# A delta-rule attention with a low-rank mixer on one core: fronts by token tile, other transfer times in the order model, and a new order

## The chip, the cores and the metric

The kernel runs on one core of a Trainium2 chip. A core has five engines that each work through their own queue of instructions in order: TensorE (PE, matrix multiply; PEld is its weight load), VectorE (DVE), ScalarE (ACT), GpSimd (POOL) and SyncE (SP). They wait for one another by semaphores. Transfers between the chip's memory (HBM) and the on-chip memory (SBUF) are issued by SP, ACT and POOL and carried by 16 DMA engines. Results of matmuls land in PSUM. The metric is the device time of one execution in microseconds.

## The reference

Four batches, eight heads, 768 positions, 48 numbers per head. The delta rule gives `x`, a mixer with a rank-32 token mix and a two-layer channel mix gives the output. Everything is float32; `U`, `V`, `w_ch1`, `w_ch2` come as float64 and are read by the kernel as pairs of 32-bit words.

```python
for t in range(S):
    kt, vt, bt = (k_n[:, :, t], v[:, :, t], beta[:, :, t, None])
    y[:, :, t] = np.einsum('bhd,bhde->bhe', q[:, :, t], state)
    v_old = np.einsum('bhde,bhd->bhe', state, kt)
    state = state + bt[:, :, :, None] * np.einsum('bhd,bhe->bhde', kt, vt - v_old)
...
h = xt @ U @ V                       # x: (4, 768, 384), heads side by side
u = x + h.transpose(0, 2, 1)
ch = np.maximum(u @ w_ch1, 0.0) @ w_ch2   # 384 -> 1536 -> 384
return (u + ch).astype(np.float32)
```

## The kernel before

**Delta rule.** The work is cut into eight units `n`: unit `2b` is the first half (384 positions) of batch `b`, unit `2b+1` the second, each of six chunks of 64 positions. A unit is loaded by `load` (L361 to L391, its issues at L379: k, q, v and a second copy z of some keys, in pieces of 72 KB; for units 2 to 7 half of the pieces go through POOL's queue). `grams` turns keys and queries with TensorE transposes (L475), copies them (L490) and multiplies them (L502); `blocks` solves small triangular systems on VectorE (L584, then pairs of L593 and L599, then L606 and L615) and joins the blocks with small matmuls (L649, L663, L689, L692, L707, L710), with a correction on VectorE (L667). `norms` scales by the key norms and by v (L458). Two units share each of two places in SBUF (`slot0`, `slot1`), so unit n+2 can be loaded only when unit n is done.

**Recursion.** `recur(b)` runs the twelve chunks of a batch one after the other: `prepare` (L808, L819), then for every chunk pb (L857), z (L870, VectorE), the state's increment (L885) and the state s (L895, VectorE), and beside this the outputs (L772, L786), which ScalarE puts into `X` (L756).

**Mixer.** For each batch the 768 positions go in three channel groups `i` of 256 positions, two token tiles `c` of 128 each. `front(b, i)` makes `u`: once per batch T (L1180, with a copy `tt`, L1186), then H (L1198), an addition on VectorE (L1202), transposes (L1207) and a copy to `ut` (L1209). `wide(b, i)` then multiplies by w_ch1 (L1288, called W1 below; six pairs of blocks of features), applies the relu (L1231) and multiplies by w_ch2 (L1328) in seven products instead of eight, with sums on VectorE (L1251, L1258) and the results added to `X` (L1264). The last batch has its first layer done in seven products too (`quick`, L1085). `load_weights` brings in 14 slices of the weights as 64-bit words (L967) and converts each with five VectorE operations (L989 to L1017) and one of ScalarE (L974); the sums of w_ch2 (L925) follow the last two slices.

**What sets the order.** The program is written as many small parts (Python generators), each yielding the operations that it wants next. `run` keeps a model of the engines' clocks while the program is built: among the parts that can go on, it takes the one that comes soonest, and among those about equally soon the one with the smaller rank. The result is a fixed order of instructions in each engine's queue; on the chip nothing is chosen any more. Three things enter: the costs that the parts give with their operations, the landing times that `landing` works out for transfers, and the ranks, which the calls of `begin` give and the table `PLACES` overrides by name.

Of the kernel before, what the change touches and what calls it, by code (L numbers as in the profile page):

```python
# [19 lines left out]
GT = 256  # L20
# [6 lines left out]
def kernel(  # L27
# [66 lines left out]
    def dve(n):  # L94
        return (n + 151) / 960.0

    def act(n):
        return 0.16 + n / 1200.0
# [14 lines left out]
    def emitted(key, after=0.0):  # L113
        done[key] = state["now"] + after
        for i in awaited.pop(key, ()):
            missing[i].discard(key)
            if not missing[i]:
                woken.append(i)

    def landing(packets, each=0.0235):  # L120
        state["hw"] = max(state["hw"], state["now"] + 1.0) + packets * each / 16
        return state["hw"] + 0.4 - state["now"]

# [14 lines left out]
            waits[i] = s  # L138

    PLACES = """  # L140
    add_up b1 i1 45.09; blocks n3 111.0; blocks n4 92.42; blocks n6 79.19
    front b1 i2 64.0; front b2 i2 68.2; grams n1 i1 1.0; grams n3 i0 53.42
    grams n3 i1 -4.5; grams n4 i0 45.18; joins n0 h1 45.17; joins n1 h0 15.27
    joins n2 h0 -4.0; joins n2 h1 7.5; joins n5 h1 18.5; joins n6 h0 60.13
    joins n6 h1 68.5; joins n7 h1 62.0; last_sum b0 i2 80.69; load n0 nameq halves(0, 1) 75.0
    load n0 namez halves(0, 1) 3.5; load n1 namez halves(0, 1) 92.5; load n5 namek halves(0, 1) 49.53; load n5 namez halves(0, 1) 92.89
    load n6 namek halves(0, 1) 68.35; load_beta u0 51.5; load_beta u1 90.62; load_weights 88.45
    norms n1 113.0; norms n2 108.5; norms n3 19.33; norms n5 46.0
    outputs b0 c0 94.0; outputs b0 c3 15.7; outputs b0 c5 84.5; outputs b1 c6 56.12
    outputs b2 c0 87.54; outputs b2 c5 58.09; outputs b3 c0 -10.5; outputs b3 c1 51.03  # L150
    outputs b3 c4 81.5; outputs b3 c6 78.5; prepare n0 h0 99.5; prepare n0 h1 78.37
    prepare n1 h0 80.0; prepare n2 h0 -1.5; prepare n2 h1 6.5; prepare n3 h0 8.5
    prepare n5 h0 7.5; prepare n5 h1 44.42; prepare n6 h1 43.06; products n0 i0 j0 97.01
    products n0 i0 j1 82.0; products n0 i1 j1 110.0; products n1 i1 j1 53.69; products n2 i0 j1 73.87
    products n3 i0 j1 31.11; products n4 i0 j0 55.59; products n4 i0 j1 57.63; products n4 i1 j0 57.63
    products n5 i1 j1 3.5; products n6 i0 j1 100.7; products n6 i1 j0 73.37; products n6 i1 j1 47.56
    products n7 i1 j0 59.09; products n7 i1 j1 86.0; recur b0 31.68; recur b1 19.99
    recur b3 22.0; seed n6 -8.0; start i1 113.77; wide b0 i0 65.24
    wide b0 i2 73.0; wide b1 i2 115.5; wide b2 i1 76.0
    """  # L160
    PLACES = dict(x.strip().rsplit(" ", 1) for x in PLACES.replace("\n", ";").split(";") if x.strip())

# [106 lines left out]
    def pair(x):  # L269
        return P[:, BANK["pair"][x] : BANK["pair"][x] + 2]  # L270
# [90 lines left out]
    def load(n, name, halves):  # L361
        kn, _, _, _, qn, vn, _, kz = units[n]
        t, src = dict(k=(kn, k), q=(qn, q), v=(vn, v), z=(kz, k))[name]
        b, hf = divmod(n, NU)
        yield need(("rec", n - 2), *[("x", b - 1, UC * hf + c) for c in range(UC)])
        if name == "v":
            yield need(("turned", n))
        if name == "k" and n == 0:
            e = "sp" if halves == (0,) else "act"
        else:  # L370
            e = "sp"
        for g in halves:
            if n >= NU and g:
                e = "pool"
            queue = dict(sp=nc.sync, act=nc.scalar, pool=nc.gpsimd)[e]
            for s in range(1, 4, 2) if name == "z" else range(4):
                to = dict(k=s, q=s, v=s % 2 * 2 + s // 2, z=s // 2)[name]
                yield op(e, 0.65, port=False)
                queue.dma_start(  # L379
                    out=t[half(1 - g if name == "z" else g), :, to, 0:D],  # L380
                    in_=src[b, 4 * g + s, hf * UC * L : (hf + 1) * UC * L, :].rearrange(
                        "(c t) d -> t c d", t=L
                    ),
                )
                after = landing(384)
                if name == "z" or s % 2:
                    emitted((name, n, g, s // 2), after)
        if len(halves) == 1 and halves[0]:
            yield op("act", 1.6)
            nc.scalar.sqrt(warm, warm)  # L390
# [162 lines left out]
    def halves(t, split):  # L553

        size = BK // split
        flat = t.rearrange("p a b -> p (a b)")[:, 0 : split * size * (BK + (split > 1))]
        return flat.rearrange("p (u x) -> p u x", u=split)[:, :, 0 : size * BK].rearrange(
            "p u (a b) -> p u a b", b=BK
        )[:, :, :, 0:size]
# [371 lines left out]
    def load_weights():  # L931
# [14 lines left out]
        def start(i):  # L946
            _, src, kind = slices[i]
            n = size(i)
            before = max([x for x in range(i) if where[x] == where[i]], default=-1)
            yield need(("started", i - 1), ("freed", before), *[("joined", 0)] * (where[i] == 2))  # L950
            to = wides[where[i]][:, 0 : 2 * n]
            landed[i] = to.rearrange("p (n two) -> p n two", two=2)
            src = src.bitcast(I32)
            if kind == "c":
                pieces = [(to.rearrange("p (c r) -> p c r", c=NB), src.rearrange("(c p) r -> p c r", c=NB))]
            elif kind == "a":
                to = to.rearrange("p (t f x) -> p t f x", t=KT, f=2)
                pieces = [(to[:, :, f], src[:, :, f]) for f in range(2)]
            elif kind == "f":
                to = to.rearrange("p (a f d) -> p f a d", a=2, f=2)  # L960
                pieces = [(to[:, f], src[f]) for f in range(2)]
            else:
                pieces = [(to[quarter(j)], src) for j in range(128 // R)]
            e, queue = ("pool", nc.gpsimd) if i < 1 else ("sp", nc.sync)
            for to, of in pieces:
                yield op(e, 0.6, port=False)
                queue.dma_start(out=to, in_=of)  # L967
            emitted(("started", i))
            emitted(("wide", i), landing(256, 0.13) + 0.6)

        def raised(i, power):
            cost = 0.16 + size(i) * 0.001
# [197 lines left out]
    def front(b, i):  # L1170
        yield need(
            ("front", *before(b, i)), *[("wide", *before(*before(b, i)))] * (b < LAST),
            ("weights", 1), *[("x", b, c) for c in range(NC)],
        )
        x = X[:, b % 2]
        if i == 0:
            o = yield op("pe", 0.8, "T", take="pair", words=24)
            p_t = one(o)[:, 0:DM]
            for c in range(NB):
                nc.tensor.matmul(  # L1180
                    p_t[R * (c % 4) : R * (c % 4) + R], u_sb[:, c], x[:, c],
                    start=(c < 4), stop=(c + 4 >= NB),
                )
            yield op("dve", dve(384), give=[("pair", o)])
            tts[b] = mix.tile([128, DM], FP32, name="tt", bufs=1)
            nc.vector.tensor_copy(out=tts[b], in_=p_t)  # L1186
        tt = tts[b]
        cs = list(range(i * GT // 128, (i + 1) * GT // 128))
        if b < LAST:
            ut = uts[b, i] = mix.tile([128, KT, GT], FP32, name="ut")  # L1190
        else:
            ut = ut_last[:, :, GT * i : GT * i + GT]

        at = slice(cs[0], cs[-1] + 1)
        o = yield op("pe", 1.3, "F", take="pair", words=8)
        p_h = pair(o)[:, :, 0:DM]
        for m, c in enumerate(cs):
            nc.tensor.matmul(  # L1198
                p_h[:, m], v_sb[:, c * 128 : (c + 1) * 128], tt, start=True, stop=True
            )  # L1200
        yield op("dve", dve(768), give=[("pair", o)])
        nc.vector.tensor_tensor(out=x[:, at], in0=x[:, at], in1=p_h, op=ALU.add)  # L1202
        o = yield op("pe", 0.84, "F", take="pair", words=12, flow=0.64)
        p_u = pair(o)[:, :, 0:DM].rearrange("p m (t n) -> p m t n", t=KT)
        for m, c in enumerate(cs):
            for t in range(KT):
                nc.tensor.transpose(p_u[:, m, t], x[:, c, t * 128 : (t + 1) * 128], ident)  # L1207
        yield op("act", act(768), give=[("pair", o)])
        nc.scalar.copy(ut.rearrange("p t (m n) -> p m t n", m=NT), p_u)  # L1209
        emitted(("front", b, i), 0.1)  # L1210

    def reserve():
# [180 lines left out]
```

## Time and profile before

| | us |
|---|---|
| median of three runs (615.25 to 617.24) | 617.05 |
| the profiled execution | 622.36 |
| its span, first to last instruction | 620.6 |
| PE busy in the span | 584.3 (94%) |
| DVE busy | 418.3 (67%) |
| ACT busy | 235.6 (38%) |
| POOL busy | 81.5 (13%) |
| mean TensorE clock | 0.929 of full |

The profile is of one execution. Matmuls overlap in the array, so a busy PE need not be at its peak; a float32 matmul appears as two records in the trace. "Idle before" is the time an engine stood still ahead of an instruction, with what ended it. Of the time, the chain of waits gives 84% to TensorE, 7% to VectorE and 2% to transfers.

### The profile page before, as it was taken

The page shows a single profiled execution, that of the slowest core. Times are in us where ns is not written, and L with a number is a line of the kernel's source. Part 1 is how long each engine was busy: PE and PEld are TensorE (multiplying, and loading weights), DVE is VectorE, ACT ScalarE, POOL GpSimd, SP SyncE. Part 2 cuts the span into 40 slices and gives each one's busy share as a digit, 9 for nine tenths or more (in the row PEclk, how much of TensorE's full clock was granted, in tenths as well). Part 3 has the DMA queues.
Part 4 walks back from the last instruction along what each step waited for, and adds up shares of the span by engine and source line. Part 5 has one row for each costly group of instructions (what it writes and reads, how often), then busy time and mean ns, then how long its engine had stood idle before and what let it go on. Part 6 is the DMA issues. An engine that isn't in the chain of part 4 may idle for free.

```text
span 620.6 us, 23281 instructions
## 1 busy us (share of the span) xinstructions
PE 584.3 (94%) x10452; PEld 502.8 (81%) x10452; DVE 418.3 (67%) x1000; ACT 235.6 (38%) x462; POOL 81.5 (13%) x145
## 2 busy tenths in 40 slices
PE   5767968899999999999999999999999999999997
PEld 4666967689889889788988978988989878755997
DVE  6968979688988817899887359968972235132542
ACT  4735654651044174246327323353134131244000
POOL 3001006410000230151025032010010000000000
PEclk9766565799999999999999999999999999999999
DMA  6560549940000240370034043000000000000001
GB/s 125 107 160 5 170 154 201 207 107 2 27 5 3 61 65 4 69 131 4 3 74 91 3 96 57 11 29 3 3 28 2 27 2 2 25 2 0 6 36 36
DMA packets 72293, 33.26 MB, mean 54 GB/s; under 512 B 59649, under 2 KB 70657, under 8 KB 72193
## 3 DMA queue, kind: packets, MB, share of 16 engines
q1 hardware_dynamic: 66400, 24.98, 18.1%
q0 software_dynamic: 4192, 6.49, 4.9%
q8 instruction: 82, 1.34, 0.9%
q10 hardware_dynamic: 1600, 0.30, 0.3%
q14 instruction: 19, 0.15, 0.1%
HBM read 27.03 MB, written 4.72 MB: 51 GB/s over the span
## 4 chain that ended last, share of the span: by engine, by line
PE 84%; DVE 7%; issue 3%; ACT 2%; DMA 2%; SPq 2%; DVEq 0%; ACTq 0%
PE P L1328 27%; PE P L1288 23%; PE P L1085 7%; PE P L502 4%; PE P L475 3%; PE P L1198 3%; PE P L857 3%; DMA slot<-in_k_dram 2%; PE P L808 2%; PE P L819 2%; PE P L885 2%; PE P L772 2%; SPq L379 2%; PE P L1207 1%; PE P L786 1%
## 5 line engine op out<-in xcount | busy, mean ns | idle before, releaser
L1288 PE MATMUL P<-ut,w_sb 128*128 128x256 f32 x648 | 153.8, 386 | 0.0
L1288 PEld LDWEIGHTS P<-ut,w_sb 128*128 128x128 f32 x648 | 119.6, 191 | 19.0 <-issue 1.9
L1328 PE MATMUL P<-w_sb,hs 128*128 128x192 f32 x540 | 95.1, 330 | 0.0
L1328 PEld LDWEIGHTS P<-w_sb,hs 128*128 128x128 f32 x540 | 87.3, 190 | 1.6
L599 DVE TENSOR_TENSOR xt<-xt,prod 128x112 f32<-128x112 f32 (+21 forms) x200 | 64.5, 323 | 6.9
L1264 DVE TENSOR_TENSOR X<-X,P 128x192 f32<-128x192 f32 x84 | 29.6, 352 | 58.4 <-PE P L1328 57.3
L756 ACT COPY X<-P 64x192 f32<-64x192 f32 x96 | 30.1, 314 | 101.9 <-PE P L786 99.7
L593 DVE TENSOR_TENSOR prod<-gs,xt 128x112 f32<-128x112 f32 (+21 forms) x200 | 63.9, 320 | 4.5
L1231 ACT ACTIVATE hs<-P 128x512 f32<-128x512 f32 x54 | 32.2, 597 | 82.0 <-PE P L1288 78.6
L1328 PE MATMUL P<-w_sb,S 128*128 128x192 f32 x288 | 50.2, 329 | 0.0
L1328 PEld LDWEIGHTS P<-w_sb,S 128*128 128x128 f32 x288 | 46.7, 190 | 0.5
L475 PE MATMUL P<-ident,slot 128*128 128x128 f32 x192 | 31.5, 314 | 11.2 <-DMA slot<-in_k_dram 7.4
L870 DVE TENSOR_TENSOR z<-slot,P 128x192 f32<-128x192 f32 x44 | 15.5, 353 | 35.2 <-PE P L857 32.2
L728 ACT COPY slot<-zz 32x384 f32<-32x384 f32 x64 | 32.5, 509 | 14.9 <-DVE X L1264 8.6
L475 PEld LDWEIGHTS P<-ident,slot 128*128 128x128 f32 x192 | 25.9, 162 | 14.6 <-issue 8.1
L502 PEld LDWEIGHTS P<-slot 48*64 48x64 f32 x1536 | 28.8, 151 | 6.9 <-ACT slot L490 3.2
L502 PE MATMUL P<-slot 48*64 48x64 f32 x1536 | 32.4, 238 | 1.7 <-ACT slot L490 1.4
L1085 PE MATMUL P<-slot,w_sb 128*128 128x384 f32 x96 | 33.3, 486 | 0.0
L379 POOL DMA_DIRECT2D slot<-in_k_dram x36 | 23.6, 669 | 66.8 <-PE P L885 66.0
L1328 PE MATMUL P<-w_sb,slot 128*128 128x192 f32 x180 | 30.1, 326 | 0.0
L1328 PEld LDWEIGHTS P<-w_sb,slot 128*128 128x128 f32 x180 | 29.4, 190 | 0.5
L490 ACT COPY slot<-P 128x768 f32<-128x768 f32 x30 | 23.5, 801 | 16.5 <-PE P L475 14.4
(143 smaller groups left out, 888.1 us busy)
## 6 DMA issues: line engine op xcount, KB each, us to landing
out_dram<-X SPq DMA_DIRECT2D x22, 192.0 KB, 1.8
slot<-in_k_dram SPq DMA_DIRECT2D x56, 72.0 KB, 3.8
X<-in_moe_w_ch_dram SPq DMA_DIRECT2D x10, 384.0 KB, 5.1
wide<-in_moe_w_ch_dram SPq DMA_DIRECT2D x10, 384.0 KB, 5.3
slot<-in_q_dram SPq DMA_DIRECT2D x40, 72.0 KB, 3.7
slot<-in_v_dram SPq DMA_DIRECT2D x40, 72.0 KB, 3.2
slot<-in_k_dram POOLq DMA_DIRECT2D x36, 72.0 KB, 4.5
slot<-in_q_dram POOLq DMA_DIRECT2D x24, 72.0 KB, 5.2
```

Source lines behind the costliest of these rows:

```text
L379: queue.dma_start(out=t[half(1 - g if name == "z" else g), :, to, 0:D], in_=src[b, 4 * g + s, hf * UC * L : (hf + 1) * UC * L, :].rearrang ...
L475: nc.tensor.transpose(p_t[:, c // 3, c % 3], t[:, c, 2 * j : 2 * j + 2].rearrange("p s d -> p (s d)"), ident,)
L502: nc.tensor.matmul(p_g[half(g ^ (par * i)), par, c], kq[rows, c, j, 0, half(g)], kq[rows, c, j, i, half(g)], start=True, stop=True,)
L593: nc.vector.tensor_tensor(out=prod, in0=gb[:, :, j : j + 1, j + 1 :].to_broadcast([128, split, m, w]), in1=xb[:, :, 0:m, j : j + 1].to_bro ...
L599: nc.vector.tensor_tensor(out=xb[:, :, 0:m, j + 1 :], in0=xb[:, :, 0:m, j + 1 :], in1=prod, op=ALU.subtract,)
L728: nc.scalar.copy(pg[quarter(i), :, at, :, a : a + BK], cut(zc, h)[quarter(i)].rearrange("p r (c j) t -> p r c j t", j=2),)
L756: nc.scalar.copy(x[half(c % 2), c // 2, 4 * D * g : 4 * D * (g + 1)].rearrange("p (j r d) -> p r j d", r=2, d=D), states(p_y)[half(g)],)
L1085: nc.tensor.matmul(to, w, t, start=start, stop=stop, skip_group_check=True)
L1231: nc.scalar.activation(hs[:, fs[0] : fs[1] + 1 : fs[1] - fs[0]], p_f, ACTF.Relu)
L1264: nc.vector.tensor_tensor(out=to, in0=to, in1=p, op=ALU.add)
L1288: nc.tensor.matmul(p_f[:, fs.index(f)], w1_sb[:, y, 256 * t + 128 * fs.index(f) :][:, 0:128], ut[:, t], start=(t == 0), stop=(t == KT - 1),)
L1328: nc.tensor.matmul(p_o, a[:, f], w2_sb[:, w, f], start=(first and f == 0), stop=(f == HF - 1), skip_group_check=True,)
```

## The change

Three edits. First, `front` handles each token tile by itself: one H matmul, one addition of 384 columns, three transposes and one copy of 384 columns, each tile in a PSUM bank of its own, as two parts that the order model may place apart (before: both tiles in one go, with one addition and one copy of 768). Second, the model gets other times of transfers: 0.0215 in place of 0.0235 us per packet of a load of q, k or v, 0.45 or 0.15 us added by queue; and for the weights 0.095 per packet and piece in place of 0.13 per slice. Third, the whole table of ranks is another one.

```diff
-    def landing(packets, each=0.0235):
+    def landing(packets, each=0.0215):
         state["hw"] = max(state["hw"], state["now"] + 1.0) + packets * each / 16
...
-                after = landing(384)
+                after = landing(384) + (0.45 if e == "pool" else 0.15)
...
                 queue.dma_start(out=to, in_=of)
+                after = landing(256, 0.095)
             emitted(("started", i))
-            emitted(("wide", i), landing(256, 0.13) + 0.6)
+            emitted(("wide", i), after + 0.2)
...
-        at = slice(cs[0], cs[-1] + 1)
-        o = yield op("pe", 1.3, "F", take="pair", words=8)
-        p_h = pair(o)[:, :, 0:DM]
-        for m, c in enumerate(cs):
+        def block(c):
+            o = yield op("pe", 0.65, "F", take="pair", words=4)
+            p_h = one(o)[:, 0:DM]
             nc.tensor.matmul(
-                p_h[:, m], v_sb[:, c * 128 : (c + 1) * 128], tt, start=True, stop=True
+                p_h, v_sb[:, c * 128 : (c + 1) * 128], tt, start=True, stop=True
             )
-        yield op("dve", dve(768), give=[("pair", o)])
-        nc.vector.tensor_tensor(out=x[:, at], in0=x[:, at], in1=p_h, op=ALU.add)
-        o = yield op("pe", 0.84, "F", take="pair", words=12, flow=0.64)
-        p_u = pair(o)[:, :, 0:DM].rearrange("p m (t n) -> p m t n", t=KT)
-        for m, c in enumerate(cs):
+            yield op("dve", dve(384), give=[("pair", o)])
+            nc.vector.tensor_tensor(out=x[:, c], in0=x[:, c], in1=p_h, op=ALU.add)
+            o = yield op("pe", 0.56, "F", take="pair", words=6, flow=0.32)
+            p_u = one(o)[:, 0:DM].rearrange("p (t n) -> p t n", t=KT)
             for t in range(KT):
-                nc.tensor.transpose(p_u[:, m, t], x[:, c, t * 128 : (t + 1) * 128], ident)
-        yield op("act", act(768), give=[("pair", o)])
-        nc.scalar.copy(ut.rearrange("p t (m n) -> p m t n", m=NT), p_u)
+                nc.tensor.transpose(p_u[:, t], x[:, c, t * 128 : (t + 1) * 128], ident)
+            at = c * 128 - i * GT
+            yield op("act", act(384), give=[("pair", o)])
+            nc.scalar.copy(ut[:, :, at : at + 128], p_u)
+            emitted(("ut", b, c))
+
+        for c in cs:
+            begin(block(c), 2)
+        yield need(*[("ut", b, c) for c in cs])
         emitted(("front", b, i), 0.1)
...
     PLACES = """
-    add_up b1 i1 45.09; blocks n3 111.0; blocks n4 92.42; blocks n6 79.19
-    front b1 i2 64.0; front b2 i2 68.2; grams n1 i1 1.0; grams n3 i0 53.42
...
+    add_up b1 i0 84.69; block b0 i0 c0 76.5; block b0 i0 c1 76.5; block b0 i2 c4 76.5
+    block b0 i2 c5 76.5; block b1 i2 c4 75.8; block b2 i1 c2 29.12; block b2 i2 c4 75.5
...
     """
```

In the built programs all five queues change their order. SP's first transfers are k and z of unit 0, q 0, k 1, two pieces of q 1, v 0, the rest of q 1, z 1, v 1 (before: k and z 0, k 1, q 1, q 0, one piece of z 1, v 1 and v 0). On TensorE, the first W1 matmuls stand ahead of the turnings of unit 3 (before: behind part of them), and the blocks of unit 2 start after 18 W1 matmuls (before: after the first group's 36 and its second layer). On VectorE, eleven of the 14 weight slices and all but one operation of a twelfth are converted ahead of the last z of batch 0 (before: ten), and the blocks of unit 2 come ahead of the last two slices (before: behind them).

More of the change, by code (lines that the diff above doesn't have):

```diff
@@ L140 @@
     PLACES = """
-    add_up b1 i1 45.09; blocks n3 111.0; blocks n4 92.42; blocks n6 79.19
-    front b1 i2 64.0; front b2 i2 68.2; grams n1 i1 1.0; grams n3 i0 53.42
[L143 to L158, printed above, removed]
@@ L159 @@
-    wide b0 i2 73.0; wide b1 i2 115.5; wide b2 i1 76.0
+    add_up b1 i0 84.69; block b0 i0 c0 76.5; block b0 i0 c1 76.5; block b0 i2 c4 76.5
+    block b0 i2 c5 76.5; block b1 i2 c4 75.8; block b2 i1 c2 29.12; block b2 i2 c4 75.5
+    blocks n0 6.0; blocks n3 104.37; blocks n4 82.29; blocks n5 81.0
+    diagonals n1 h0 81.93; diagonals n1 h1 81.43; diagonals n2 h0 80.8; diagonals n3 h1 83.5
+    front b2 i0 88.5; grams n2 i0 79.44; grams n2 i1 20.0; grams n4 i1 13.93
+    grams n5 i1 74.28; grams n6 i0 50.5; grams n6 i1 125.5; grams n7 i0 13.35
@@ new lines @@
+    joins n2 h0 21.37; joins n2 h1 28.04; joins n4 h0 -9.5; joins n5 h0 68.5
+    joins n6 h0 -10.5; last_sum b0 i0 75.28; load n0 nameq halves(0, 1) 20.0; load n1 namek halves(0, 1) 81.79
+    load n1 nameq halves(0, 1) 81.79; load n1 namez halves(0, 1) 81.79; load n2 namez halves(0, 1) 4.5; load n6 nameq halves(0, 1) 80.0
+    load n7 nameq halves(0, 1) 12.0; load_beta u0 41.97; load_beta u1 3.5; load_weights 76.54
+    norms n1 1.5; norms n2 73.5; norms n5 94.69; norms n6 3.0
+    norms n7 0.4; outputs b0 c0 76.55; outputs b0 c1 84.97; outputs b0 c10 21.43
@@ new lines @@
+    outputs b0 c9 76.87; outputs b1 c3 80.0; outputs b1 c7 6.0; outputs b1 c8 63.11
+    outputs b2 c0 -11.0; outputs b3 c0 70.16; outputs b3 c5 83.5; outputs b3 c6 95.5
+    part n1 h1 88.2; prepare n1 h0 73.0; prepare n1 h1 79.38; prepare n2 h0 15.63
+    prepare n3 h0 23.0; prepare n4 h0 94.28; prepare n4 h1 94.28; prepare n5 h1 19.5
+    products n0 i0 j0 63.5; products n0 i0 j1 67.5; products n0 i1 j1 63.5; products n1 i0 j0 70.44
+    products n1 i1 j0 70.44; products n1 i1 j1 70.44; products n2 i0 j0 90.0; products n2 i1 j1 76.04
@@ L160 @@
+    products n3 i0 j0 7.0; products n3 i1 j1 87.88; products n4 i1 j0 29.19; products n5 i1 j0 79.0
+    products n5 i1 j1 80.0; products n6 i1 j0 94.5; products n7 i1 j0 86.0; products n7 i1 j1 86.0
+    recur b0 73.0; recur b1 14.12; recur b2 -5.82; reserve 6.33
+    start i1 100.5; weight_sums 48.97; wide b1 i2 10.87; wide b2 i0 128.0
+    wide b2 i1 71.5; wide b2 i2 99.06
     """
```

## The prediction

> **What bounds the kernel now.** I read the busy table in 40 slices first, then the same by stage, then the chain of waits, then single rows of the timeline.
>
> The first view is part 2 of the page: each digit is the busy share of 15.5 us in tenths.
>
> ```profile
> ## 2 busy tenths in 40 slices
> PE   5767968899999999999999999999999999999997
> ...
> DVE  6968979688988817899887359968972235132542
> ...
> PEclk9766565799999999999999999999999999999999
> DMA  6560549940000240370034043000000000000001
> ```
>
> TensorE has gaps and a lowered clock in the first eight slices and neither after them. The second view gives busy time by stage (us, then busy and count of PE, PEld, DVE, ACT, POOL; clock; DMA share; GB/s).
>
> ```profile
> 93.00:108.50 15.50, 12.71 (x374) 11.10 (x370) 14.73 (x27) 6.44 (x15) 9.90 (x16) 0.50 1.03 202
> 108.50:126.00 17.50, 15.57 (x211) 10.57 (x212) 10.96 (x18) 10.68 (x17) 6.54 (x10) 0.70 1.07 197
> 126.00:160.00 34.00, 34.00 (x232) 31.13 (x231) 30.59 (x65) 10.29 (x16) 2.59 (x4) 0.99 0.17 43
> 160.00:205.00 45.00, 44.63 (x1324) 38.94 (x1323) 39.19 (x96) 15.66 (x33) 2.62 (x5) 1.00 0.04 13
> ```
>
> Up to 108 us VectorE is the bound (14.73 of 15.50), doing the delta rule of batch 0 and the conversion of the weights. From 108.5 to 126 nobody is full except the DMA engines. From 126 on TensorE is full. The chain of waits names what is waited for in between:
>
> ```profile
> 109.30 9.40 DMA slot<-in_k_dram
> 118.69 0.14 issue
> 118.83 0.84 PE P L475 x6
> 119.67 0.74 PE P L1207 x6
> 120.42 2.77 PE P L502 x96
> 123.19 2.86 PE P L1198 x4
> 126.04 1.80 PE P L1288 x6
> ```
>
> The turning (L475) of unit 3's keys waits for a transfer, and the first front (L1207, then L1198) stands behind it in TensorE's queue.
>
> I sum TensorE's queue at undisturbed prices from the chain: 1.29 for six records of L1288, 1.95 for twelve of L1328, 1.29 for four of L1198, 1.31 for twelve of L475, 41.28 for L1085's 128, 0.71 for 48 of L502, 0.23 for 16 of L857; 0.15 to 0.20 more at each change between the large matmuls and the small ones (L1328 x12 is 2.15 behind a small group, 1.95 behind its own kind). That makes 532.4 us. The last matmul ends at 617.3, so TensorE stands 85.0 behind its own work; 78.0 of this is there when the first L1288 group ends (127.84, with 49.8 of work done), 79.1 at 160 of work, and only 6 come after. So the change is worth what it does to the first 78, plus what it adds or takes in the rest.
>
> **Two pages of the Trainium skill.** "TensorE: Matmul & The Clock Gate", section "What's actually happening", says that the array runs at half rate until it has been busy for a window of some 3.4 us. The trace agrees: the 96 records of L502 take 2.77 in the chain at 120.42 and 1.56 at 161.36, L1198 2.86 against 1.29. I go by the trace, and count a late clock as 1 to 3 us of possible loss. "VectorE: DVE Perf Modes", section on the TRN2 errata, says that many small operations pay a fixed cost each that a large one pays once. The rows agree for the split of the front:
>
> ```profile
> L1202 DVE TENSOR_TENSOR X<-X,P 128x768 f32<-128x768 f32 x12 | 11.4, 952 | 10.7 <-PE P L1198 10.3
> ...
> L1094 DVE TENSOR_TENSOR slot<-slot,P 128x384 f32<-128x384 f32 x18 | 10.0, 554 | 27.4 <-PE P L1085 27.4
> ```
>
> **The front by token tile.** Two additions of 554 in place of one of 952: +0.16 us of VectorE per front, 1.9 over twelve. Two ScalarE copies of 479 (the 128x384 copies of L1103) for one of 801 (L1209): +0.16, 1.9 over twelve. TensorE's matmuls are the same. ScalarE is busy 38%, so its part costs nothing; VectorE's costs only where VectorE is the bound, up to three fronts: 0.5 us. On the other side a front exposed to the end shortens: before 1.29 + 0.95 + 0.65 + 0.80 = 3.7; now the first tile's addition runs under the second's matmul, 1.29 + 0.55 + 0.33 + 0.48 = 2.65. In the full stage the trace has few fronts exposed: the chain has L1202 once (262.74, 0.96), and the group of L1207 behind it is 0.7 late, another 0.2, the L502 behind 0.3. I take 1.0 us off for these; bounds 0 and 1.5.
>
> **The new order, first 65 us.** The new transfer times put no instruction in and change none; they act only through the order, which the two built programs show. SP's issues of a 72 KB piece follow each other by 0.67 with a few jumps of 0.85, and land 2.5 to 3.5 later. v of unit 0 moves from place 41-48 to 27-34, issued by 24.7, landed by 27.5; before, VectorE waited for it:
>
> ```profile
> 38.57 1.36 DVE L458 TENSOR_TENSOR slot<-slot,norm_rows 128x1152 f32<-128x1152 f32 x1 [4.70 <-DMA slot<-in_v_dram]
> ```
>
> These 4.7 us go. What is late next: q of unit 1, now behind it at places 35-40, lands at about 32, and its turning stands ahead of unit 0's joins (L649, L663: some 1.5 each per half at the low clock), so VectorE's correction (L667) comes 2.9 later than VectorE reaches it; then v of unit 1, issued last (39.2, landed 41.9), holds L458 by another 2 to 2.8. Summing VectorE's queue at its start-to-start distances, VectorE is 10.0 behind its work at 40 us before, and by this 9.2 after it; 9.6 with the wait for unit 1's joins. So the gain is about 1 us, not 4.7.
>
> **Up to the end of batch 0's recursion.** VectorE's work ahead of its last z (L870) is 92.8 before and 99.5 after: nine conversion operations more stand ahead of it (eleven weight slices and all but one operation of the twelfth, where it was ten), of 0.47 to 0.98 us each, start to start: 6.8. From 62 us to there VectorE lost 4.8 before (late pb, two pauses of TensorE's issue of 1.1 to 1.6, L1007 behind ScalarE). Nothing in the new order removes these, so I keep 4.8: 9.6 + 4.8 + 99.5 = 113.9, against 108.4.
>
> **From there to full speed.** Put in its copy (L756, 1.0), the low-clock T group (L1180, 2.7) and tt (0.6), the new front's first addition stands behind L584 (1.9): 121.6. Its second pair of additions stands behind 4.3 us more of VectorE's queue: 125.9. The transposes and nine W1 matmuls (0.7 + 3.9) then end at 130.7, with 54.8 of work done: 75.9 behind, where before it was 78.0. The reason is that unit 3's turnings now stand behind twelve W1 matmuls, so that the 9.40 wait of the chain is off the path, and all weight slices but two are converted.
>
> **The coupled stage.** For this VectorE is kept nearly full until 160 of TensorE's work. It is then 16.5 behind its own queue. Unit 2's blocks now come before the last two weight slices: their transpose ends at 120.6 + 16.5 = 137.1, where TensorE would come at 59.9 + 75.9 = 135.8: 1.3 lost. Slice 13 is due at 139.5 + 17 = 156.5 against 80.8 + 77.2 = 158.0: in time. The first z of batch 1 (144.2 + 17.4 + 0.5) is 0.5 late; its later steps have 0.3 to 5 us in hand. That leaves 77.7, against 79.1 before at 160 of work: -1.4. POOL's memsets and SP's stores wait in the same queues as loads of units 4 to 7, whose keys are due 2 to 5 us ahead of their turnings; nothing of that costs in the sum, and up to 2 us if landings take the 7 to 9 us of the stage at 110.
>
> **Sum.** TensorE's work -0.15; start -1.4; fronts in the full stage -1.0, given back 0.5 of VectorE's longer fronts in the coupled stage: -2.05. The profiled execution has a span of 620.6 and took 622.4; the change makes it 618.6 and 620.3. The median of the runs shown is 617.05, 0.9% lower with the same order: 615.0.
>
> **Rivals.**
> (a) No change that can be told (0.3%, 1.85 us, either way): VectorE's larger queue ahead of the last z (+5.5) is paid for by the transfer off the path, but the clock is still low at 126 us, so that the first W1 matmuls lose 1.5. For it: the half clock up to 126.9; against it: fewer gaps between 115 and 126. 616.5.
> (b) Slower: VectorE becomes the bound. Each us that VectorE is later than 113.9 at its last z goes straight to the end, since the coupled stage has only 0.3 to 1.5 us in hand where it had 2 to 6. It decides from 2.1 us on. If the recursion loses 8 in place of 4.8 and two more joins are late by 1, it is 113.9 + 3.2 + 2: +3.2 net, 620.2. For it: VectorE at 14.73 of 15.50 us before the last z, so that a loss has no idle time to go into; against: the same recursion lost 4.8 before.
> (c) The gain is larger: the waits that I put at q and v of unit 1 (2.9 and 2.8) don't come, because VectorE reaches these steps later anyway. Then 4 us more are saved, of which the coupled stage passes on some 2.5: 612.5.
>
> **Chances.** Forecast and (c), both faster: 0.43 (0.29 and 0.14); (a) 0.28; (b) 0.29. (c) reaches 610 when all its 4 us and one of the fronts' come through; some two thirds of (b) lie below 621.5. Between these the chance is about 0.8, and the bounds of the fronts (0 to 1.5) and of late landings (2) lie inside.
>
> **What would show it.** Right: L458's 4.7 gone; no key transfer in the chain near 110; first L1288 group by 125 us, TensorE without gaps from 131 on; VectorE 9s between 110 and 230. Wrong: gaps of TensorE between 131 and 240 released by VectorE (L870, L615, L895), a half clock after 128, or a chain that goes over VectorE up to 230.

## The result, and the profile after

| | before | after |
|---|---|---|
| median of four runs, us | 616.25 (615.25 to 617.24) | 622.83 (622.47 to 623.17) |
| profiled execution, us | 622.36 | 622.47 |
| its span, us | 620.6 | 620.8 |
| mean TensorE clock | 0.929 | 0.942 |

The change makes the kernel slower by 1.0%: the ratio of the times is 1.0096, with an interval of 1.0075 to 1.0116. The forecast was 615.0 with a range from 610 to 621.5. The two profiled executions differ by only 0.1 us: the one of before stood 5 us above the other runs of its kernel, and the one of after does not. This turned out to be a large part of the story.

The busy table of the changed kernel (tenths in slices of 15.5 us), to be laid beside the one of before:

```profile
## 2 busy tenths in 40 slices
PE   5697787799999999999999999999999999999997
...
DVE  6859998999999888589838988886312125332542
...
PEclk9958555999999999999999999999999999999999
```

VectorE is nearly full from the fourth slice to the thirteenth (46 to 202 us), where before had a six, a seven and more eights among its nines. The clock is at full speed one slice earlier: the eighth slice (108.5 to 124) has a 9 where before has a 7. By stage (us; busy and count of PE, PEld, DVE, ACT, POOL; clock; DMA share; GB/s):

```profile
93.00:108.50 15.50, 11.90 (x361) 10.77 (x356) 12.83 (x23) 6.76 (x14) 6.92 (x11) 0.50 1.01 218
108.50:126.00 17.50, 14.36 (x351) 10.68 (x351) 16.04 (x32) 9.98 (x19) 9.59 (x15) 0.94 0.89 184
126.00:160.00 34.00, 33.52 (x789) 28.65 (x788) 32.34 (x70) 16.79 (x30) 4.40 (x7) 1.00 0.20 37
```

From 108.5 to 126 VectorE is now the full engine (16.04 of 17.50, before 10.96), and TensorE the one with gaps (14.36, before 15.57), though its clock is 0.94 instead of 0.70. The chain of waits says the same: the key transfer of 9.40 us near 110 is gone, and where TensorE stood in the chain of before, the chain now goes over VectorE, for most of the time up to 162 us and hardly behind it. TensorE itself hardly stands still from 128 to 240 us: its waits of more than 0.15 us add up to 0.8 us there.

```profile
121.45 0.90 PE P L506 x48
122.52 0.93 DVE slot L537 x2
...
125.56 1.01 DVE X L1206 x2
126.73 0.23 DVE xt L603
```

The second pair of front additions (L1206) stands in VectorE's queue behind masked copies and norms of unit 2, and behind it come the pairs of L597 and L603 of unit 2's blocks. (Line numbers from the loads on are 3 to 9 higher than in the kernel before.)

### The profile page after: what moved, and what is told of

The parts are those of the page before. It is cut to its first block, busy times and chain, and to the rows that moved or that the text cites. A ratio compares the mean times of both kernels' runs of the same rounds, so it can differ in the third digit from the quotient of the medians.

```text
span 620.8 us, 23348 instructions
## 1 busy us (share of the span) xinstructions
PE 585.2 (94%) x10452; PEld 505.1 (81%) x10452; DVE 420.3 (68%) x1012; ACT 237.1 (38%) x474; POOL 82.0 (13%) x145
## 3 DMA queue, kind: packets, MB, share of 16 engines
q0 software_dynamic: 4192, 6.49, 4.8%
## 4 chain that ended last, share of the span: by engine, by line
PE 75%; DVE 16%; ACT 3%; issue 3%; DMA 2%; SPq 1%; DVEq 0%; ACTq 0%
PE P L1337 27%; PE P L1297 20%; PE P L1090 7%; PE P L506 3%; DVE prod L597 2%; PE P L1202 2%; DVE xt L603 2%; PE P L861 2%; PE P L479 2%; PE P L889 2%; SPq L383 1%; PE P L776 1%; PE P L823 1%; DVE power L1012 1%; PE P L812 1%
## 5 line engine op out<-in xcount | busy, mean ns | idle before, releaser
L1273 DVE TENSOR_TENSOR X<-X,P 128x192 f32<-128x192 f32 x84 | 29.6, 353 | 71.7 <-PE P L1337 71.0
L603 DVE TENSOR_TENSOR xt<-xt,prod 128x112 f32<-128x112 f32 (+21 forms) x200 | 64.6, 323 | 6.9
L597 DVE TENSOR_TENSOR prod<-gs,xt 128x112 f32<-128x112 f32 (+21 forms) x200 | 64.0, 320 | 4.7
L760 ACT COPY X<-P 64x192 f32<-64x192 f32 x96 | 30.1, 313 | 75.3 <-PE P L790 74.4
L1099 DVE TENSOR_TENSOR slot<-slot,P 128x384 f32<-128x384 f32 x18 | 10.0, 554 | 27.4 <-PE P L1090 27.4
```

Of the source, the lines that this page charges most:

```text
L597: nc.vector.tensor_tensor(out=prod, in0=gb[:, :, j : j + 1, j + 1 :].to_broadcast([128, split, m, w]), in1=xb[:, :, 0:m, j : j + 1].to_bro ...
L603: nc.vector.tensor_tensor(out=xb[:, :, 0:m, j + 1 :], in0=xb[:, :, 0:m, j + 1 :], in1=prod, op=ALU.subtract,)
L760: nc.scalar.copy(x[half(c % 2), c // 2, 4 * D * g : 4 * D * (g + 1)].rearrange("p (j r d) -> p r j d", r=2, d=D), states(p_y)[half(g)],)
L1273: nc.vector.tensor_tensor(out=to, in0=to, in1=p, op=ALU.add)
```

## The experiments

I sum TensorE's queue at undisturbed prices, as in the prediction, and call "behind" how much later than this sum TensorE is. In e2_joins_first, e2_q_first, e2_late_conv and all kernels of e3 and e4 the order is written out: they have all the instructions of the kernel named, but the picks of the order model were recorded, a few moved, and the list put in the place of the model's choice. Line numbers in them are 80 to 82 higher than in the kernel named. Each profile is of one execution, so "behind" has the scatter of single executions.

| kernel | median us (runs) | ratio to before, interval | behind at the end of the first W1 group | at 160 of work | at the end |
|---|---|---|---|---|---|
| before, profile of the prediction | 616.25 (4) | 1 | 78.0 | 79.1 | 85.0 |
| after, first profile | 622.83 (4) | 1.0096, 1.0075 to 1.0116 | 76.7 | 79.1 | 85.3 |
| e1_before | 617.25 (22) | 1.0005, 0.9988 to 1.0021 | 73.8 | 75.2 | 81.1 |
| e1_after | 622.96 (6) | 1.0101, 1.0074 to 1.0128 | 79.0 | 81.4 | 88.1 |
| e1_front | 644.27 (6) | 1.0463, 1.0432 to 1.0493 | 71.2 | 73.4 | 104.2 |
| e1_landing | 650.54 (6) | 1.0559, 1.0528 to 1.0590 | 81.2 | 83.1 | 108.0 |
| e2_split | 615.98 (22) | 0.9985, 0.9970 to 1.0001 | 70.7 | 71.7 | 77.0 |
| e2_joins_first | 622.27 (6) | 1.0086, 1.0054 to 1.0119 | 76.6 | 79.0 | 85.5 |
| e2_q_first | 620.97 (9) | 1.0070, 1.0046 to 1.0093 | 73.7 | 76.1 | 83.1 |
| e2_late_conv | 627.57 (6) | 1.0170, 1.0138 to 1.0201 | 74.4 | 84.2 | 90.6 |
| e3_start_before | 629.46 (6) | 1.0184, 1.0145 to 1.0223 | 75.3 | 86.7 | 93.8 |
| e3_start_after | 630.33 (6) | 1.0206, 1.0169 to 1.0242 | 77.3 | 85.0 | 91.9 |
| e3_both | 621.15 (17) | 1.0079, 1.0058 to 1.0100 | 76.1 | 78.4 | 84.8 |
| e4_v0_first | 614.29 (15) | 0.9969, 0.9954 to 0.9984 | 69.9 | 71.6 | 76.9 |

**Both kernels once more.** Nothing is edited; the question was whether the profile of before shows an unusual execution (theory A), or whether taking a profile costs the 5 us (theory B).

> The kernel before once more, profiled again. Its profiled execution took 622.4 us while its timed ones took 615.3 to 617.2. Theory A (that execution was an unusual one, with the key transfer of unit 3 and the half clock up to 126.9 us lying badly; the usual start is some 6 us shorter): timed 616 +- 1 again, and at least in the executions near 616 a span near 614.5 with the first L1288 group ended by 122 us in place of 127.8 and a mean granted clock of 0.94 or more. Theory B (the profile itself costs this kernel 6 us): timed 616, profiled 622 again, the first L1288 group ended at 127 to 128.

> The changed kernel once more. Theory A: 622.5 to 623.2 timed and profiled alike, the first wide matmuls ending where they did (W1 group after the second front near 131 us), since its start waits on VectorE's queue and not on a transfer. Theory B: the profile's time above the timed one by some us here too; equal times in both speak against B.

The new profile of before has a span of 616.7 and a first W1 group that ends at 123.6 instead of 127.8. Its chain of waits has no key transfer in it, and reads at the same place:

```profile
117.23 1.31 PE P L475 x12
118.54 0.75 PE P L1207 x6
119.29 1.56 PE P L502 x96
120.85 1.49 PE P L1198 x4
122.34 1.29 PE P L1288 x6
```

Against the chain in the prediction: L502 x96 1.56 instead of 2.77, L1198 1.49 instead of 2.86, L1288 1.29 instead of 1.80. In the first profile the clock went to full at 113.3, fell back to half at 120.1 (such a fall is called a relapse below) and returned at 126.9; here it rises at 114.8 and stays. That is 3.1 of the 4.2 us, and the wait for keys (1.93 ahead of L475, none here) and what follows from it are the other 1.1. The 9.40 in the first chain is the transfer from its issue to its landing; TensorE stood still for 1.93 of it:

```profile
118.83 0.84 PE L475 MATMUL P<-ident,slot 128*128 128x128 f32 x6 [1.93 <-DMA slot<-in_k_dram]
```

Behind the first W1 group both executions lose the same (85.0 - 78.0 = 7.0, and 81.1 - 73.8 = 7.3). So A holds in this, that the first profile shows an unusual execution: of the 120 timed runs of this kernel in the experiments only one took as long (622.86), and half took less than 617. Its figures all missed, though: the span is 616.7 (expected 614.5), the group ends at 123.6 (by 122), and the mean clock is 0.922 (0.94 or more), lower than in the slower first profile. The mean clock over the span does not tell a good start from a bad one; where the low clock lies does. B falls: in the 13 other profiled executions of all kernels the time lies 1.6 us below to 2.3 us above the median of the same kernel, by 0.2 on average.

The second profile of the changed kernel took 625.3, 2.3 above its median, where A expected 622.5 to 623.2. This execution has a relapse of its own: the clock falls to half from 114.2 to 121.0, where it stayed full in the first. The T group of the first profile, then of e1_after:

```profile
117.68 1.49 PE L1185 MATMUL P<-X,u_sb 128*32 128x384 f32 x12 [0.43 <-ACT X L760]
```

```profile
118.97 2.48 PE L1185 MATMUL P<-X,u_sb 128*32 128x384 f32 x12
```

So both kernels have executions with and without a relapse between 114 and 127 us, and are best compared like with like (though the two relapses do not hit the same work). Without one, the changed kernel is 2.9 us further behind at the end of the first W1 group (76.7 against 73.8), 3.9 at 160 of work and 4.2 at the end; with one, it is 1.0, 2.3 and 3.1. Within one order, what a start loses comes out at the end nearly whole: 4.2 of start and 3.9 at the end for before, 2.3 and 2.8 for the changed kernel.

**Each half of the edit alone**, with the ranks of before: the fronts by tile (e1_front), or the new transfer times (e1_landing).

```diff
 # e1_front: only block(c) in front(), as in the diff of the change
 # e1_landing: only
-    def landing(packets, each=0.0235):
+    def landing(packets, each=0.0215):
-                after = landing(384)
+                after = landing(384) + (0.45 if e == "pool" else 0.15)
+                after = landing(256, 0.095)
-            emitted(("wide", i), landing(256, 0.13) + 0.6)
+            emitted(("wide", i), after + 0.2)
```

> Only the fronts by token tile, with the transfer times and ranks of before; the model then places everything a little differently. If the split front is what costs, about 622; theory A (the new ranks' longer VectorE queue ahead of the last z costs): 616 to 619, with the last z of batch 0 near 108 us and not near 115.

> Only the new transfer times, with the fronts and ranks of before. The ranks were found for the other times, so the order is off by some steps: 616 to 622. If the new transfer times alone make the order bad, 622 or more with the waits at the same places as in the changed kernel (L671, the correction of unit 0, near 40 to 45 us).

Both are far slower than anything expected of them, and neither tells what the edit is worth, since the model answers with another order throughout. e1_front has a better start than the kernel before (71.2 behind), and then loses some 18 us between 160 and 200 of work: from 220 to 260 us TensorE is busy 35.95 of 40 us at a clock of 0.87, where the changed kernel has 39.70 at 1.00. A table of ranks fits one set of costs.

**The front's cut without a new order** (order of before; each addition and each copy replaced in its place by two).

```diff
-        nc.vector.tensor_tensor(out=x[:, at], in0=x[:, at], in1=p_h, op=ALU.add)
+        for m, c in enumerate(cs):
+            nc.vector.tensor_tensor(out=x[:, c], in0=x[:, c], in1=p_h[:, m], op=ALU.add)
...
-        nc.scalar.copy(ut.rearrange("p t (m n) -> p m t n", m=NT), p_u)
+        for m in range(NT):
+            nc.scalar.copy(ut[:, :, 128 * m : 128 * m + 128], p_u[:, m])
```

> The kernel before with its order kept instruction for instruction; only each front's addition and copy are cut into two of one token tile each. If the split costs what its rows say (0.16 us of VectorE and 0.16 of ScalarE per front, mostly under other work): within 2 us of 617.2. If the split front is a part of the 5.7 us that the change lost: 619 or more.

The ratio is 0.9985 and its interval touches 1. So the cut costs nothing that can be told and may bring up to 0.3%; the 1.0% lies in the new order. The additions of all twelve fronts keep VectorE busy for 12.4 us, 1.0 more than the 11.4 of before:

```profile
L1203 DVE TENSOR_TENSOR X<-X,P 128x384 f32<-128x384 f32 x24 | 12.4, 548 | 7.6 <-PE P L1198 7.3
```

**Three edits of the changed order.** Theory D: in the changed order VectorE is the bound up to some 230 us, so that idle time of VectorE ahead of the front is passed on to the end. Theory E: the weight conversion that stands ahead of batch 0's last z is what delays it. (The lines say what moved in the queues; they are not code.)

```diff
 # e2_joins_first, order of after: TensorE, and VectorE
-q of unit 1 turned (L479 x12); joins of unit 0 (L653, L667 x96 each)
+joins of unit 0; q of unit 1 turned
-scaling of unit 1 by v (L462) ahead of the last step of unit 1's blocks
+behind it
 # e2_q_first, order of after: SP
-q 1 (2 pieces); v 0 (8); q 1 (6)
+q 1 (8 pieces); v 0 (8)
 # e2_late_conv, order of after: VectorE, with the ScalarE steps that belong to it
-weight slices 10 and 11 (ten operations, 7.8 us) ahead of the last z of batch 0
+behind the second front, ahead of slice 12
```

> The changed kernel's order, with two steps moved: the turning of unit 1's queries (L479) comes behind unit 0's joins (L653, L667) on TensorE, and unit 1's scaling by v (L462) behind its substitution on VectorE. Theory D (in the changed order VectorE is the bound up to some 230 us, so each us that it stands still early comes out at the end): the 6.5 us wait of L671 near 36 to 42 us shrinks by 4 to 6, and the time by as much, to 617 to 619. Rival E (the start is lost later, at the conversion put ahead of the last z): the wait shrinks and the time stays at 622 to 623.

> The changed kernel's order; only on SP's queue the six other pieces of unit 1's q come ahead of unit 0's v, so that they land some 5 us earlier. Theory D: the turning of unit 1's queries ends by 30.5 in place of 34.4, the wait of L671 falls from 6.5 to about 3, against 1 us at L462 which now waits for v; 620 to 621. If the low clock in the joins is what makes L671 late and not q's landing: 622 to 623.

> The changed kernel's order, with two weight slices (ten VectorE operations, 7.8 us) moved from ahead of batch 0's last z to behind the second front and to ahead of the next slice. Rival E: T, the fronts and the first wide matmuls come 6 to 7 us earlier and the time falls by 4 or more, to 618. Theory D: they come earlier too, but TensorE then waits for VectorE at unit 2's joins and at the second layer, and the time stays within 2 us of 622.8.

e2_q_first gave D what it asked for: VectorE's idle time up to the second pair of front additions fell from 17.2 to 14.2 us, the first W1 group is 3.0 less behind, and the span is 618.6 against 620.8. The time, 620.97, is within D's 620 to 621; it is 1.9 us less than the changed kernel, with intervals that overlap. The gain is seen in the correction L671 (L753 in this kernel): its wait fell from 6.49 to 1.66, while 1.11 of waiting for v came at L462 (L544), as expected.

```profile
38.02 0.54 DVE L753 SCALAR_TENSOR_TENSOR zz<-P,upper_rows,zz 128x96 f32<-128x96 f32 x2 [1.66 <-issue]
```

e2_joins_first speaks against D: its time, 622.27, is not D's 617 to 619 but the 622 to 623 of the rival. It took 2.0 us of idle away at the same place and gave them back: at the second front's additions VectorE's idle time is 17.1, as in the changed kernel. At the halved clock that TensorE had from 113.8 to 117.3, VectorE's L601 (L519 in the changed kernel) waited there 1.06 and 0.73 for ScalarE, which waited for TensorE. In the changed kernel these waits are 0.41 and 0.53 at full clock, and 1.03 and 0.96 in e1_after, whose clock was at half there.

e2_late_conv made E fall (627.57, where E said 618), but D's figure missed too (within 2 us of 622.8). With 7.8 us of work taken away, the last z came only 2.5 us earlier (112.9 instead of 115.4), since the conversion had filled holes of the recursion that are now open (z is L956 here, s L981):

```profile
111.19 0.35 DVE L981 TENSOR_TENSOR s<-s,P 128x192 f32<-128x192 f32 x1 [2.87 <-PE P L971]
112.93 0.35 DVE L956 TENSOR_TENSOR z<-slot,P 128x192 f32<-128x192 f32 x1 [1.38 <-PE P L943]
```

The same 7.8 us then had to be done in the coupled stage, where VectorE has nothing to spare. TensorE's waits from 130 to 175 us (engine and line, what for; us, times, longest):

```profile
PE P L735 <- DVE zz L692: 2.9, 1, 2.9
PE P L775 <- DVE zz L753: 1.5, 1, 1.5
```

With two smaller ones these are 5.2; in the changed kernel TensorE's waits for VectorE in that stretch are 0.6 in all. TensorE goes from 74.4 to 82.4 behind by the start of the second layer. Not all of that is waiting: in the wait of 2.9 the clock fell to half, from 137.4 to 144.2, and the four groups run in it took 2.6 us longer than the same groups in the changed kernel, such as these six W1 records (1.56 there):

```profile
139.59 2.93 PE L1379 MATMUL P<-ut,w_sb 128*128 128x256 f32 x6
```

**Start and rest exchanged, and two edits together.** In the two hybrids the order up to the first W1 group is that of one kernel, and what is left follows in the order of the other; both have the instructions of the changed kernel. D against rival F: the order of the rest holds the loss.

```diff
 # e3_start_before: start of before, rest of after
-unit 2's second products, norms and first block steps ahead of the first W1 group
+behind it (unit 3's first turning and products ahead of it)
 # e3_start_after: start of after, rest of before: the reverse
 # e3_both: e2_joins_first and e2_q_first in one
```

> All instructions of the changed kernel, in a hybrid order: up to the first group of W1 matmuls the order of the kernel before (its fronts cut in two per tile in place), everything after that in the order of the changed kernel. Theory D (what the changed order loses, it loses ahead of the first W1 group, and VectorE carries it to the end): the first W1 group ends 71 to 74 us behind the sum of TensorE's queue instead of 76.7 to 79.0, and the time is 616.5 to 619. Rival F (the start is not what decides; the changed order of the rest, where the lag grows by 8.6 to 9.1 us instead of 6.3 to 7.3, holds the loss, or brings any start to the same end): 621.5 to 623.5, with a lag that grows by 11 or more behind the first W1 group.

> The mirror of the other hybrid: the order of the changed kernel up to its first group of W1 matmuls, and from there on the order of the kernel before. Theory D: the first W1 group ends 76 to 79 us behind, and 6 to 8 follow: 620 to 622.5. Rival F: the order of the kernel before makes up for the late start (lag growth of 4 or less): 615.5 to 618.

> The changed order with two of the edits above together: the remaining pieces of unit 1's q ahead of unit 0's v on SP's queue, and unit 0's joins ahead of the turning of unit 1's q on TensorE (with unit 1's v scaling behind the substitution on VectorE). Theory D: both take idle time from VectorE ahead of unit 0's correction, and what is left at the second pair of the front's additions decides: 14 us of idle or less, and 618.5 to 620.5. Rival F: 621 to 623, as the changed kernel itself.

The hybrids took 629.46 and 630.33, outside what either theory said: they lose 9.6 and 4.8 us right at the seam. In e3_start_before TensorE, having done its first W1 group, waits for VectorE, and its clock is at half from 128.1 to 138.3, in which 18 records of W1, nine matmuls, take 6.23 (4.05 in the changed kernel):

```profile
127.76 1.36 PE L587 MATMUL P<-slot 48*64 48x64 f32 x48 [2.60 <-DVE X L1287]
...
133.89 6.23 PE L1378 MATMUL P<-ut,w_sb 128*128 128x256 f32 x18
```

They don't separate D from F. One thing can be read: from the second layer on, the rest of before loses no less (9.8) than the rest of after (8.9), so the rest of before does not by itself make up for a late start. e3_both is no better than e2_q_first alone, and its 621.15 lies in F's range and 0.65 above D's: its clock went back to half from 113.4 to 116.8, L601's waits are 0.98 and 0.87, and 2.4 of the 3.0 us of idle that e2_q_first had saved are back at the second front's additions.

**A version for the start of before** (e2_split's order; unit 0's v ahead of the rest of unit 1's v, as early as its buffer is free, and two masked copies moved into a hole of VectorE).

```diff
 # SP
-v 1 (7 pieces); v 0 (8); v 1 (1)
+v 1 (5 pieces); v 0 (8); v 1 (3)
 # VectorE
-correction L667; scaling by v L458; transpose; ...; L533 x2 of unit 0's last products
+L533 x2 of unit 0's last products; correction L667; scaling by v L458; transpose; ...
```

> The order of the kernel before with its fronts cut in two per tile (as in the run with the split fronts), and two edits ahead of batch 0's recursion: on SP's queue unit 0's v goes ahead of the rest of unit 1's v as early as its buffer allows (five pieces of unit 1's v stay ahead of it, 1.3 us earlier), and on VectorE the two masked copies of unit 0's last products (0.98 us) move into the hole ahead of the first correction (3.24 us of waiting in the profile of the split fronts). No instruction is added or taken out. By theory D, in the form that VectorE's idle time ahead of the recursion is passed on to the end in the order of before too, 2.1 us of idle go (1.15 of the v wait, 0.98 of the hole) and the time is 613.0 to 615.0, below both kernels. Rival: the recursion behind it, whose steps wait for TensorE, takes the gain back, as it did where unit 0's joins came first; then it is 615.5 to 617.

The time is 614.29, as expected by D, the ratio 0.9969 (0.9954 to 0.9984): below both kernels, and the only one here whose interval lies below 1. How much of it the two moves bring beyond the cut fronts stays open: the interval of e2_split overlaps, and the two profiled spans are 612.6 and 612.7. Of the 2.1 us of idle, 0.9 went. The copies went into the hole, but the wait for v stayed as it was (1.15 in e2_split):

```profile
38.22 1.36 DVE L538 TENSOR_TENSOR slot<-slot,norm_rows 128x1152 f32<-128x1152 f32 x1 [1.12 <-DMA slot<-in_v_dram]
```

## Why the prediction was wrong

**The step that failed most: the baseline.** The prediction took "78.0 of this is there when the first L1288 group ends" from one execution as a property of the order, forecast 75.9 for the new order against it, and then carried the result to the median: "the median of the runs shown is 617.05, 0.9% lower with the same order: 615.0". The 78.0 contained a relapse of the clock; a second execution of this order, nearer to its median, has 73.8 (e1_before). It makes no difference that it scaled: 617.05 less the 2.05 is 615.0 as well. The error is the term "start -1.4", a gain over an execution that had lost some 4 us which most executions of that order do not lose. With 75.2 at 160 of work instead of 79.1, the same sum reads +2.5 for the start, -0.5 for fronts, -0.15 for TensorE's work: 1.85 us slower instead of 2.05 faster. So of the 7.8 us between 615.0 and 622.83 the baseline is 3.9. The start of the new order is another 1.4 and the fronts 0.8 (both below). The last 1.7 are not in the two profiles that are compared here: the one of before (618.44) lies above its median, the one of after (622.47) below. The text gave the warning sign itself (622.36 against 617.05) and did not use it.

**The reason for the gain fell with it.** That "the 9.40 wait of the chain is off the path" was to pay for VectorE's larger queue. In e1_before that wait isn't in the chain, so taking it off the path pays for nothing; and in the first profile it was a wait of 1.93, not of 9.40.

**A row read at the wrong clock.** The prediction priced the joins of unit 0 at "some 1.5 each per half at the low clock", so that the correction L671 would come 2.9 late. Those 1.5 were full-clock rows. The timeline of TensorE in the profile of the prediction, then the same two lines in e1_before:

```profile
29.70 1.53 PE L649 MATMUL P<-zz,hs 64*64 64x16 f32 x48
31.64 1.51 PE L663 MATMUL P<-zz,S 64*64 64x16 f32 x45 [0.41 <-ACT zz L654]
```

```profile
30.64 2.70 PE L649 MATMUL P<-zz,hs 64*64 64x16 f32 x48
33.75 2.63 PE L663 MATMUL P<-zz,S 64*64 64x16 f32 x45 [0.41 <-ACT zz L654]
```

That execution's clock was full from 28.0 to 34.8. In the changed kernel the q of unit 1 lands at 31.4 (forecast: about 32), its turning and then both halves of the joins run at half clock, and VectorE waits 6.49 instead of 2.9:

```profile
31.42 2.93 PE L479 MATMUL P<-ident,slot 128*128 128x128 f32 x12 [5.45 <-DMA slot<-in_q_dram]
34.27 5.31 PE L653 MATMUL P<-zz,hs 64*64 64x16 f32 x96
```

```profile
42.25 0.54 DVE L671 SCALAR_TENSOR_TENSOR zz<-P,upper_rows,zz 128x96 f32<-128x96 f32 x2 [6.49 <-issue]
```

The 2 to 2.8 of waiting for unit 1's v, put behind it, then didn't come, as VectorE was late already; rival (c) had that half. Net, by the sum of the prediction, VectorE is 11.8 behind its work there instead of 9.6, and the last z ends at 115.7 instead of 113.9.

**A hit by luck.** These 1.8 us do not show at the second pair of the front's additions, which come at 125.6 (forecast 125.9). The terms that the prediction lists behind the last z (1.0, 2.7, 0.6, 1.9) add up to 120.1 and not to the 121.6 that it goes on with, so 1.5 us without a term made good for the late z. The terms themselves were off both ways: T started some 2.0 behind the end of z instead of 1.0, and took 1.49 at full clock instead of 2.7 at half. Of the 1.8 us, 0.8 are there at the end of the first W1 group (76.7 behind, forecast 75.9) and 1.4 at 160 of work (79.1, forecast 77.7). Rival (b) had the sign right, and the chain over VectorE and e2_q_first speak for its engine. That each us goes "straight to the end" is not shown ahead of the first W1 group, and its own cause, more loss in the recursion, didn't come (4.4 idle there, forecast 4.8).

**Fronts in the full stage: -1.0, given back 0.5.** Between 160 of work and the end the changed kernel loses 6.2 us (forecast 5.4; before 5.9). The cut alone in the order of before loses 5.3 there, where e1_before loses 5.9, so the mechanism is possible, but the new order doesn't show it. Start 1.4 and fronts 0.8 make the 2.2 by which the profiled sum was short.

**What was right.** L458's wait for v is gone; there is no key transfer in the chain near 110; the first W1 group ends 76.7 behind (75.9), though its first six records end at 126.9 and not by 125; TensorE has no gaps to speak of from 131 on. VectorE is at nine tenths or more from 108 to 202, and at eight up to 233, where nines were forecast up to 230. The cut of the front costs next to nothing, as the rows of 952 and 554 gave it; the rule on fixed costs ("VectorE: DVE Perf Modes", section on the TRN2 errata) agrees with the 1.0 us more that VectorE is busy in e2_split, though the prediction, adding up lengths, had 1.9. Of the signs of being wrong, only the chain over VectorE came, and that up to 162. The profiled execution of the changed kernel is therefore the forecast one some 2 us later, measured against a kernel before that started 4 us better in its second profile than in its first.

**What stays open.** Which of the many exchanged steps makes the start of the new order 3 us later than that of before (76.7 against 73.8, executions without a relapse), and the 1.0 that follows up to 160 of work. The place of unit 1's q behind unit 0's v is a part of it, if the 1.9 us of e2_q_first are taken as they stand. VectorE's nine conversion operations more ahead of the last z are in it, but putting ten operations later did not bring the time back, and the hybrids failed at their seams.

## What to carry to other kernels

Before a profile becomes the baseline, lay its time beside the timed runs; if it is 5 us off, find where these are before forecasting a difference of 2, and take a second profile. A gain over the profiled execution is not a gain over the median. Read each row's clock before using its duration: the same 48 records of L649 took 1.5 or 2.7 us in two executions of one program. Where one engine's queue is full, moving its work later was no gain here, since the later stage had no idle time of that engine, and an edit to an order found by search has to be tried with the order held fixed, or the search run anew.

## What the runs showed of the hardware

TensorE's clock in the start differs between executions of one program: full-clock windows of before were 10.9 to 14.3, 21.1 to 24.5, 28.0 to 34.8, 48.4 to 51.8, 79.2 to 82.6 and 113.3 to 120.1 in one profile, 9.0 to 12.4, 22.6 to 26.0 and 60.2 to 63.6 in another, then full from 114.8 on. All lengths are multiples of 3.4 us. The Trainium skill ("TensorE: Matmul & The Clock Gate", section "What's actually happening") describes such a free-running window and calls its effect variable between runs. What I had not expected is its weight this late: a relapse of two windows at 120 us cost 3.1 us, 0.5% of the kernel, which is more than the edit was forecast to bring.

Nor does it take a window without work. Leaving out the first 100 us and the last 10, the clock fell to half twelve times in the 14 traces, and in the 3.41 us just ahead TensorE was busy for 24 to 73% of the time (43% in the first profile of before, from 116.7 to 120.1). In some windows with as little as 50% it stayed full, so the share alone does not decide. The two profiles of the changed kernel show how little it takes: from 110.5 to 113.9 TensorE was busy 64% in one and the clock stayed full; in the other the same work fell into a window from 110.8 to 114.2 with 55%, and the next two windows ran at half. In e3_start_before three windows at half (128.1 to 138.3) began 0.3 us after a wait of 2.60 us had ended.
